# Feeding the FFN: transposes from TensorE to DMA, layer norm on VectorE, both evacuations on ScalarE, another chunk order

## The chip, the cores and the metric

The kernel runs on one core of a Trainium2 chip. Its time is the device time of one execution in microseconds; three executions of the kernel before took 417.68 to 417.83 us, median 417.8. Lower is better. The core's engines are named as in the profile: PE is TensorE (matmuls; PEld its weight loads), DVE is VectorE, ACT is ScalarE, POOL is GpSimd, SP is SyncE, which here only issues DMAs.

## The reference

Two layers of the same pair of blocks over a sequence of 2048 rows of 512 in bf16, each block added to its input:

```python
def _A_ref(q, k, v, shift_k, ssm_k, ssm_D):      # q is the normalised x
    k_shift = sum over t of k_pad[:, t:t + S, :] * shift_k[:, ks - 1 - t]
    kv = k_shift * v
    y = irfft(rfft(kv, 2 * S) * rfft(ssm_k, 2 * S))[:S]      # a long causal convolution
    y = y + kv * ssm_D
    return q * y

def _B_ref(x, w_gate, w_up, w_down):             # F = 1792
    return (silu(x @ w_gate) * (x @ w_up)) @ w_down

x = x + _A_ref(_layernorm(x), A_k, A_v, A_shift_k, A_ssm_k, A_ssm_D)
x = x + _B_ref(_layernorm(x), B_w_gate, B_w_up, B_w_down)
# ... and both once more
```

The convolution's result y depends on k, v and the filter alone, so it is the same in both layers and is computed once.

## The kernel before, in words

The sequence is cut into four chunks of 512 rows (`c`, 0 to 3); a chunk's residual is the tile `xc`, 128 partitions by 4 rows by 512, three buffers. The work on one chunk in one layer is an `ffn(layer, c)`: 14 feature tiles `ft`, each with four gate and four up matmuls (128x128 weights, 512 columns) into two PSUM banks of the tile `pf`, six banks in all, then 4 x 14 down matmuls, whose four results are added to `xc`. ScalarE takes the gate's bank through Silu into `sg`; VectorE multiplies `sg` with the up bank straight out of PSUM into `ht`.

An FFN's input is `zT`, the layer-normalised chunk with features on the partitions. The function `prologue(layer, c)` makes it: it normalises `xc` into `n` (first layer norm, on ScalarE), multiplies by the convolution's result `Y[c]` (the tile `Yk`) and adds to `xc`, takes new statistics (`ln_stats`, on VectorE, with the power of -1/2 on GpSimd), normalises again into `z` (ScalarE), has TensorE transpose the 4 x 4 blocks of `z` into the PSUM tile `ptz`, and ScalarE copies these into `zT`. With `fine` (the first prologue alone) it goes pair of rows by pair of rows.

The convolution is done block by block through 512-point transforms written as matmuls: `spectrum_h(b)` transforms the filter (TensorE transposes `hn` into `pt`, then 16 matmuls into `pc`, two banks), `spectrum_x(b)` the shifted and multiplied input (64 small matmuls with `kTb`, then 16), VectorE forms the products of spectra (`product`, into `Z`), `fold` makes `su` of them, and `inverse(k)` is 16 matmuls on `su` whose results ScalarE copies into `Yk`.

Order: the start-up part is issued as written. From the first `ffn` on, each `ffn` takes steps of its `behind` list after every feature tile (`tick`; `BEHIND` says how many), and a scheduler then puts every engine's instructions into a fixed order ahead of time, which each engine and each DMA queue follows strictly. All loads, stores and the transposing loads of `k` go through SP's queue in order. The `plan` decides which chunk's FFN comes when and what lies behind it.

Of the kernel before, what the change touches and what calls it, by code (L numbers as in the profile page):

```python
# [30 lines left out]
def kernel(  # L31
# [41 lines left out]
    work = tc.alloc_tile_pool(name="work", bufs=2)  # L73
    psp = tc.alloc_tile_pool(name="psp", bufs=1, space=PSUM)
# [29 lines left out]
    wts = {}  # L104
# [17 lines left out]
    ident = const.tile([P, P], BF16, name="ident")  # L122
# [27 lines left out]
    def psf():  # L150
        return psp.tile([P, D], F32, name="pf", bufs=6)
# [4 lines left out]
    def mm(o, terms):  # L156
        for n, (lhsT, rhs) in enumerate(terms):
            nc.tensor.matmul(o, lhsT=lhsT, rhs=rhs, start=(n == 0), stop=(n == len(terms) - 1))  # L158
# [105 lines left out]
    PAIRS = ((0, 2), (1, 3))  # L264

    def fold(Zk, su, sl):
        lo, hi = (slice(0, 2), slice(2, 4)) if sl is None else (sl, sl + 2)
        nc.vector.tensor_add(out=su[:, lo], in0=Zk[:, lo], in1=Zk[:, hi])
        nc.vector.tensor_sub(out=su[:, hi], in0=Zk[:, lo], in1=Zk[:, hi])
# [58 lines left out]

    def normalise(dst, xc, i, o, st):
        rstd, nmr = st  # L330
        nc.scalar.activation(out=dst, in_=xc[:, i, :], func=ACT.Identity, scale=rstd[:, o:o + 1], bias=nmr[:, o:o + 1])  # L331

    zts = {}

    def ln1_stats(layer, c):
        st1[layer, c] = yield from ln_stats_g(xs[c], range(R))
# [3 lines left out]
    def prologue(layer, c, fine=False):  # L340
        xc = xs[c]
        if (layer, c) not in st1:
            yield from ln1_stats(layer, c)
        st = st1.pop((layer, c))
        zT = work.tile([P, KD, R, P], BF16, name="zT", bufs=2)
        zts[layer, c] = zT
        ns = []
        for pair in PAIRS:
            n = work.tile([P, 2, D], BF16, name="n", bufs=2)
            for o, i in enumerate(pair):  # L350
                normalise(n[:, o, :], xc, i, i, st)
            ns.append(n)
        yield

        def transposes(pair, st2):
            pt = psp.tile([P, KD, 2, P], BF16, name="ptz", tag="pc", bufs=2)
            for o, i in enumerate(pair):
                z = work.tile([P, D], BF16, name="z", bufs=2)
                normalise(z[:], xc, i, (o if fine else i), st2)
                for kd in range(KD):  # L360
                    nc.tensor.transpose(pt[:, kd, o, :], z[:, kd * P:(kd + 1) * P], ident[:])  # L361
                yield
            nc.scalar.copy(out=zT[:, :, pair[0]:pair[1] + 1:2, :], in_=pt[:])  # L363
            yield

        for pair, n in zip(PAIRS, ns):
            sl = slice(pair[0], pair[1] + 1, 2)
            nc.vector.tensor_mul(out=n[:], in0=n[:], in1=Y[c][:, sl, :])  # L368
            nc.vector.tensor_add(out=xc[:, sl, :], in0=xc[:, sl, :], in1=n[:])  # L369
            yield  # L370
            if fine:
                yield from transposes(pair, ln_stats(xc, pair))
        if not fine:
            st2 = ln_stats(xc, range(R))
            yield
            for pair in PAIRS:
                yield from transposes(pair, st2)

    def drain(*gens):
        for g in gens:  # L380
            for _ in g:
                pass
# [8 lines left out]
    def ffn(layer, c, behind):  # L391
        steps = NF + R

        def run():
            for g in behind:
                yield from g()
        g = run()
        total = BEHIND[layer, c]
        done = [0, 0]

        def tick():
            done[0] += 1
            while done[1] * (8 if total < 20 else 13) < total * done[0]:
                done[1] += 1
                if next(g, g) is g:
                    break

        xc, zT = xs[c], zts.pop((layer, c))
        hts = []
        for ft in range(NF):  # L410
            pg, pu = psf(), psf()
            mm(pg[:], [(wts["g"][:, kd, ft * P:(ft + 1) * P], zT[:, kd]) for kd in range(KD)])
            mm(pu[:], [(wts["u"][:, kd, ft * P:(ft + 1) * P], zT[:, kd]) for kd in range(KD)])
            sg = work.tile([P, L], BF16, name="sg", bufs=2)
            nc.scalar.activation(out=sg[:], in_=pg[:], func=ACT.Silu)  # L415
            ht = work.tile([P, L], BF16, name="ht", bufs=14)
            nc.vector.tensor_mul(out=ht[:], in0=sg[:], in1=pu[:])  # L417
            hts.append(ht)
            tick()
        for i in range(R):  # L420
            pd = psf()
            mm(pd[:], [(hts[ft][:, i * P:(i + 1) * P], wts["d"][:, ft, :]) for ft in range(NF)])
            nc.vector.tensor_add(out=xc[:, i, :], in0=xc[:, i, :], in1=pd[:])  # L423
# [43 lines left out]
    for par in (0, 1):  # L467
        for _ in product(0, 0, slice(par, 4, 2)):
            if par == 0:
                next(f1)  # L470
        if par == 0:
            prol = prologue(0, 0, True)
            next(prol)
        fold(Z[0], su, par)
    Z.pop(0)
    drain(inverse(0, psf, su), prol)
# [10 lines left out]
    def x_only(b):  # L487
# [51 lines left out]
```

## Time and profile before

| | us |
|---|---|
| median of three executions | 417.8 |
| the profiled execution | 417.13 |
| its span, first to last instruction | 415.3 |
| TensorE busy | 370.3 (89%) |
| VectorE busy | 301.3 (73%) |
| ScalarE busy | 178.7 (43%) |
| GpSimd busy | 19.9 (5%) |

Busy time of TensorE is that of matmuls that overlap in its pipeline: 512 columns show 0.38 us each, while the next one starts 0.216 us later. The mean granted TensorE clock was 0.979. In a row of groups stand the line, the engine, the operation, the tile written and the tiles read, their shapes, the count, then busy time and mean duration, then the engine's idle time just ahead of them and what ended most of it. In a row of the timeline stand start, length, engine, line, operation, tiles, count, and in brackets the idle time ahead.

### The profile page before, as it was taken

Reading aid. Unit: us, or ns where it says so; the run is one execution under the profiler, and the core shown is the slowest. Engines: PE = TensorE matmul, PEld = TensorE weight load, DVE = VectorE, ACT = ScalarE, POOL = GpSimd, SP = SyncE. Lnnn points to the kernel's source line nnn. Section 1 sums busy time; section 2 is a strip of 40 time slices with the busy share of each in tenths; the row PEclk is TensorE's granted clock in tenths of the full one; section 3 lists DMA queues with packets and bytes.
Section 4 is the critical chain, followed back from the end, with each engine's and each line's share of the span. In section 5 each row is a group of like instructions: output and inputs, shape, how many; then the busy total and the mean of one; then the engine's idle time right before and its main releaser. Section 6 shows DMA issues by size and latency. Waiting matters only on the chain.

```text
span 415.3 us, 5086 instructions
## 1 busy us (share of the span) xinstructions
PE 370.3 (89%) x1947; PEld 178.3 (43%) x1984; DVE 301.3 (73%) x504; ACT 178.7 (43%) x281; POOL 19.9 (5%) x27
## 2 busy tenths in 40 slices
PE   2957299888889999989998999999999998999996
PEld 2722164333334644444443634444444443444442
DVE  8797886999794799999999969968233458323331
ACT  4648437231559541429144660475136134602310
POOL 1000100000000000010010000010000000000000
PEclk9988689999999999999999999999999999999999
DMA  8992013000001040000030000000100000000001
GB/s 244 396 290 109 0 20 85 2 0 0 2 0 51 2 104 0 0 2 2 2 101 0 2 0 2 1 2 0 48 4 1 2 0 0 2 25 25 2 13 38
DMA packets 18023, 16.36 MB, mean 39 GB/s; under 512 B 10064, under 2 KB 15952, under 8 KB 18000
## 3 DMA queue, kind: packets, MB, share of 16 engines
q1 hardware_dynamic: 16272, 14.99, 11.6%
q10 hardware_dynamic: 1728, 1.05, 0.9%
q8 instruction: 15, 0.25, 0.2%
q14 instruction: 8, 0.07, 0.0%
HBM read 11.80 MB, written 2.10 MB: 33 GB/s over the span
## 4 chain that ended last, share of the span: by engine, by line
PE 46%; DVE 34%; ACT 8%; issue 5%; DMA 4%; POOL 2%; POOLq 0%; DVEq 0%; ACTq 0%
PE pf L158 38%; PE pc L158 5%; DVE bnst L317 4%; DVE ht L417 4%; DMA hn<-in_A_ssm_k_dram 4%; DVE t L252 3%; DVE t L259 3%; DVE t L250 3%; DVE Z L261 3%; ACT z L331 2%; POOL rstd L323 2%; ACT ev L183 2%; DVE n L368 2%; DVE xc L369 2%; DVE xc L423 1%
## 5 line engine op out<-in xcount | busy, mean ns | idle before, releaser
L415 ACT ACTIVATE sg<-pf 128x512 bf16<-128x512 f32 x112 | 66.4, 597 | 160.9 <-PE pf L158 125.3
L158 PE MATMUL pf<-zT,wg_sb 128*128 128x512 bf16 x435 | 115.9, 380 | 5.7 <-DVE ht L417 4.0
L158 PE MATMUL pf<-zT,wu_sb 128*128 128x512 bf16 x436 | 115.8, 380 | 0.7
L417 DVE TENSOR_TENSOR ht<-sg,pf 128x512 bf16<-128x512 bf16 x112 | 76.5, 684 | 52.7 <-PE pf L158 44.2
L158 PE MATMUL pf<-wd_sb,ht 128*128 128x512 bf16 x438 | 99.8, 379 | 1.5 <-DVE ht L417 0.9
L158 PEld LDWEIGHTS <-ht 128*128 128x128 bf16 x448 | 43.5, 98 | 53.7 <-DVE ht L417 2.4
L158 PEld LDWEIGHTS <-wg_sb 128*128 128x128 bf16 x448 | 43.2, 98 | 53.8 <-issue 7.3
L158 PEld LDWEIGHTS <-wu_sb 128*128 128x128 bf16 x448 | 43.7, 98 | 51.2 <-issue 1.1
L423 DVE TENSOR_TENSOR xc<-xc,pf 128x512 bf16<-128x512 bf16 x32 | 21.5, 687 | 32.5 <-PE pf L158 32.5
L317 DVE BATCH_NORM_STATS2 bnst<-xc 128x6 f32<-128x512 bf16 x64 | 42.3, 682 | 0.3
L323 POOL TENSOR_TENSOR rstd<-ve,nhalf 128x4 f32<-128x4 f32 (+1 forms) x17 | 18.1, 1067 | 330.4 <-DVE ve L321 317.7
L331 ACT ACTIVATE z<-xc,nmr,rstd 128x512 bf16<-128x512 bf16 x32 | 24.6, 806 | 20.7 <-DVE nmr L325 20.2
L183 ACT ACTIVATE ev<-pc 128x512 bf16<-128x512 f32 x48 | 27.0, 611 | 12.0 <-PE pc L158 11.9
L361 PE MATMUL ptz<-ident,z 128*128 128x128 bf16 x128 | 13.5, 232 | 16.2 <-ACT z L331 16.0
L331 ACT ACTIVATE n<-xc,nmr,rstd 128x512 bf16<-128x512 bf16 x32 | 24.9, 821 | 4.7 <-DVE nmr L325 4.7
L250 DVE TENSOR_TENSOR t<-X,G 128x2048 bf16<-128x2048 bf16 (+1 forms) x22 | 24.8, 1127 | 0.1
L252 DVE TENSOR_TENSOR t<-X,G 128x2048 bf16<-128x2048 bf16 (+1 forms) x22 | 24.8, 1126 | 0.0
L158 PEld LDWEIGHTS <-tab_fwd 128*128 128x128 bf16 x128 | 12.8, 101 | 20.6 <-issue 10.1
L361 PEld LDWEIGHTS <-z 128*128 128x128 bf16 x128 | 8.4, 102 | 26.8 <-ACT z L331 24.4
L158 PEld LDWEIGHTS <-kTb 128*128 128x128 bf16 x256 | 18.0, 122 | 2.8 <-issue 1.7
L363 ACT COPY zT<-ptz 128x1024 bf16<-128x1024 bf16 x16 | 16.1, 1004 | 3.1 <-PE ptz L361 3.1
L208 PE MATMUL pt<-ident,hn 128*128 128x128 bf16 x64 | 5.4, 243 | 13.0 <-DVE hn L434 8.3
(61 smaller groups left out, 250.3 us busy)
## 6 DMA issues: line engine op xcount, KB each, us to landing
xc<-in_A_q_dram SPq DMA_DIRECT2D x4, 512.0 KB, 4.5
out_dram<-xc SPq DMA_DIRECT2D x16, 128.0 KB, 1.7
wg_sb<-in_B_w_gate_dram SPq DMA_DIRECT2D x1, 1792.0 KB, 10.6
wu_sb<-in_B_w_up_dram SPq DMA_DIRECT2D x1, 1792.0 KB, 14.7
wd_sb<-in_B_w_down_dram SPq DMA_DIRECT2D x1, 1792.0 KB, 20.0
hn<-in_A_ssm_k_dram SPq DMA_DIRECT2D x3, 512.0 KB, 6.7
vt<-in_A_v_dram SPq DMA_DIRECT2D x3, 512.0 KB, 3.4
hn<-in_A_ssm_k_dram ACTq DMA_DIRECT2D x1, 512.0 KB, 3.6
```

Of the source, the lines that this page charges most:

```text
L158: nc.tensor.matmul(o, lhsT=lhsT, rhs=rhs, start=(n == 0), stop=(n == len(terms) - 1))
L183: nc.scalar.activation(out=ev[:, slot, part], in_=ps[:], func=ACT.Copy, scale=scale)
L250: nc.vector.tensor_mul(out=t1[:], in0=Xi[:, sl, 0, :], in1=Gj[:, sl, part, :])
L252: nc.vector.tensor_mul(out=t2[:], in0=Xi[:, sl, 1, :], in1=Gj[:, sl, 1 - part, :])
L317: nc.vector.bn_stats(out=st[:], in_=xc[:, i, :])
L323: nc.gpsimd.tensor_tensor(out=rstd[:], in0=ve[:], in1=nhalf[:].to_broadcast((P, n)), op=ALU.pow)
L331: nc.scalar.activation(out=dst, in_=xc[:, i, :], func=ACT.Identity, scale=rstd[:, o:o + 1], bias=nmr[:, o:o + 1])
L361: nc.tensor.transpose(pt[:, kd, o, :], z[:, kd * P:(kd + 1) * P], ident[:])
L363: nc.scalar.copy(out=zT[:, :, pair[0]:pair[1] + 1:2, :], in_=pt[:])
L415: nc.scalar.activation(out=sg[:], in_=pg[:], func=ACT.Silu)
L417: nc.vector.tensor_mul(out=ht[:], in0=sg[:], in1=pu[:])
L423: nc.vector.tensor_add(out=xc[:, i, :], in0=xc[:, i, :], in1=pd[:])
```

## The change

Four edits:

- `normalise` runs as a TENSOR_SCALAR on VectorE in place of an ACTIVATE on ScalarE, for `n` and `z` alike (32 of each in all). `n` is made pair by pair with one buffer.
- Except in the first prologue, `zT` is no longer made by TensorE and ScalarE: SP issues a transposing DMA from SBUF to SBUF for each of the four rows of `z` (28 in all, 128 KB each).
- In the FFN, ScalarE evacuates both banks, the gate's through Silu into `sg`, the up's by a copy into `ht`; VectorE multiplies two feature tiles at once, in bf16 out of SBUF, in place.
- The plan's order is (0,0), (0,1), (1,0), (1,1), (0,2), (0,3), (1,2), (1,3); before it was (0,2) ahead of (1,1). The steps behind the FFNs are dealt out anew, 40 for each of the first five.

```diff
     def normalise(dst, xc, i, o, st):
         rstd, nmr = st
-        nc.scalar.activation(out=dst, in_=xc[:, i, :], func=ACT.Identity, scale=rstd[:, o:o + 1], bias=nmr[:, o:o + 1])
+        nc.vector.tensor_scalar(out=dst, in0=xc[:, i, :], scalar1=rstd[:, o:o + 1], scalar2=nmr[:, o:o + 1],
+                                op0=ALU.mult, op1=ALU.add)
...
-        ns = []
-        for pair in PAIRS:
-            n = work.tile([P, 2, D], BF16, name="n", bufs=2)
-            for o, i in enumerate(pair):
-                normalise(n[:, o, :], xc, i, i, st)
-            ns.append(n)
-        yield
-
         def transposes(pair, st2):
-            pt = psp.tile([P, KD, 2, P], BF16, name="ptz", tag="pc", bufs=2)
+            if fine:
+                pt = psp.tile([P, KD, 2, P], BF16, name="ptz", tag="pc", bufs=2)
             for o, i in enumerate(pair):
                 z = work.tile([P, D], BF16, name="z", bufs=2)
                 normalise(z[:], xc, i, (o if fine else i), st2)
-                for kd in range(KD):
-                    nc.tensor.transpose(pt[:, kd, o, :], z[:, kd * P:(kd + 1) * P], ident[:])
+                if fine:
+                    for kd in range(KD):
+                        nc.tensor.transpose(pt[:, kd, o, :], z[:, kd * P:(kd + 1) * P], ident[:])
+                else:
+                    nc.sync.dma_start_transpose(out=zT[:, :, i, :], in_=z[:].rearrange("p (k f) -> p k f", k=KD))
                 yield
...
-        for pair, n in zip(PAIRS, ns):
+        for pair in PAIRS:
             sl = slice(pair[0], pair[1] + 1, 2)
+            n = work.tile([P, 2, D], BF16, name="n", bufs=1)
+            for o, i in enumerate(pair):
+                normalise(n[:, o, :], xc, i, i, st)
...
-        for ft in range(NF):
-            pg, pu = psf(), psf()
...
-            sg = work.tile([P, L], BF16, name="sg", bufs=2)
-            nc.scalar.activation(out=sg[:], in_=pg[:], func=ACT.Silu)
-            ht = work.tile([P, L], BF16, name="ht", bufs=14)
-            nc.vector.tensor_mul(out=ht[:], in0=sg[:], in1=pu[:])
+        for f0 in range(0, NF, 2):
+            sg = work.tile([P, 2, L], BF16, name="sg", bufs=2)
+            ht = work.tile([P, 2, L], BF16, name="ht", bufs=7)
+            for o, ft in enumerate((f0, f0 + 1)):
+                pg, pu = psf(), psf()
...
+                nc.scalar.activation(out=sg[:, o, :], in_=pg[:], func=ACT.Silu)
+                nc.scalar.copy(out=ht[:, o, :], in_=pu[:])
+                tick()
+            nc.vector.tensor_mul(out=ht[:], in0=ht[:], in1=sg[:])
...
     plan = [
         ((0, 0), [g_(x_only, 1), g_(spectrum_x, 1), g_(conv_products, 1), g_(inverse, 1),
-                  g_(prologue, 0, 1), g_(loads, 2), g_(eager, 1)]),
-        ((0, 1), [g_(prologue, 1, 0), g_(spectrum_h, 2), g_(spectrum_x, 2), g_(conv_products, 2)]),
+                  g_(prologue, 0, 1), g_(loads, 2)]),
+        ((0, 1), [g_(prologue, 1, 0), g_(eager, 1), g_(spectrum_h, 2), g_(spectrum_x, 2)]),
-        ((1, 0), [g_(inverse, 2), g_(prologue, 0, 2), g_(loads, 3), g_(eager, 2), g_(spectrum_h, 3)]),
-        ((0, 2), [g_(prologue, 1, 1), g_(spectrum_x, 3), g_(conv_products, 3), g_(inverse, 3)]),
-        ((1, 1), [g_(prologue, 0, 3)]),
+        ((1, 0), [g_(prologue, 1, 1), g_(conv_products, 2), g_(eager, 2), g_(loads, 3)]),
+        ((1, 1), [g_(inverse, 2), g_(prologue, 0, 2), g_(spectrum_h, 3), g_(spectrum_x, 3)]),
+        ((0, 2), [g_(conv_products, 3), g_(inverse, 3), g_(prologue, 0, 3)]),
...
-    BEHIND = {(0, 0): 55, (0, 1): 49, (1, 0): 45, (0, 2): 44, (1, 1): 10, (0, 3): 10, (1, 2): 10, (1, 3): 1}
+    BEHIND = {u: 40 for u, _ in plan}
+    BEHIND.update({(0, 3): 10, (1, 2): 10, (1, 3): 1})
```

What this does to the fixed orders shows at three places. The first is VectorE near the end of the first FFN, (0,0), where the products for chunk 1 end in `su`, on which TensorE's inverse waits. A row gives line, operation, tile written and tiles read, shape, and in brackets the counters that it waits for (DVE, PE, Activation for an engine, DMAHW for a DMA). Before:

```order
L259 TENSOR_TENSOR t_721<-t_721,t_722 128x2048 [waits DVE_49]
L417 TENSOR_TENSOR ht<-sg,pf 128x512 [waits PE_49,Activation_49]
L261 TENSOR_TENSOR Z<-Z,t_721 128x4x512 [waits DVE_49]
L417 TENSOR_TENSOR ht<-sg,pf 128x512 [waits PE_49,Activation_49]
L268 TENSOR_TENSOR su<-Z 128x2048 [waits DVE_49]
L269 TENSOR_TENSOR su<-Z 128x2048
```

and now:

```order
L259 TENSOR_TENSOR t_746<-t_746,t_747 128x2048 [waits DVE_49]
L261 TENSOR_TENSOR Z<-Z,t_746 128x4x512 [waits DVE_49]
L250 TENSOR_TENSOR t_1122<-X_624,G_520 128x2048
L268 TENSOR_TENSOR su<-Z 128x2048 [waits DVE_49]
L269 TENSOR_TENSOR su<-Z 128x2048
L421 TENSOR_TENSOR ht<-ht,sg 128x1024 [waits Activation_49]
```

Fewer products stand between the spectra's rows, a row of a later product has come ahead of `su`, and the seventh and last pair of feature tiles stands behind `su`. In TensorE's list, 13 of the first FFN's down matmuls now stand ahead of the inverse of chunk 1 and 43 behind it; behind these stand block 2's filter transposes, 16 filter matmuls and 27 of its shift matmuls, and only then the first gate matmul of (0,1). Before, five down matmuls stood ahead of the inverse, and block 2's spectrum came after the start of (0,1).

The second place is VectorE where `z` of chunk 1 is made, from the fourth of the residual adds (L426) that end (0,0). Now:

```order
L426 TENSOR_TENSOR xc<-xc,pf 128x512 [waits PE_49]
L331 TENSOR_SCALAR z<-xc,rstd,nmr 128x512 [waits DVE_49]
L331 TENSOR_SCALAR z<-xc,rstd,nmr 128x512
L318 BN_AGGR mv<-bnst 128x2 x2
L317 BN_STATS bnst<-xc 128x6
L317 BN_STATS bnst<-xc 128x6 [waits DVE_49]
L318 BN_AGGR mv<-bnst 128x2 [waits DVE_49]
L252 TENSOR_TENSOR t_1143<-X_624,G_520 128x2048
L318 BN_AGGR mv<-bnst 128x2 [waits DVE_49]
L256 TENSOR_TENSOR Z<-t_1142,t_1143 128x4x512 [waits DVE_49]
L331 TENSOR_SCALAR z<-xc,rstd,nmr 128x512 [waits DMAHW2_49]
L331 TENSOR_SCALAR z<-xc,rstd,nmr 128x512 [waits DMAHW3_49]
```

The first two `z` stand behind that add, which waits for the last down matmul of (0,0), and the last two wait for the DMAs that read the two `z` buffers. Before, `z` was ScalarE's, which does no residual add:

```order
L331 ACTIVATE z<-xc,nmr,rstd 128x512 [waits DVE_49]
L331 ACTIVATE z<-xc,nmr,rstd 128x512
L331 ACTIVATE z<-xc,nmr,rstd 128x512 [waits PE_49,Activation_49]
L363 COPY zT<-ptz 128x8x128 [waits PE_49]
L331 ACTIVATE z<-xc,nmr,rstd 128x512 [waits Activation_49]
```

There the third `z` waited for TensorE's transposes; now it waits for a DMA, and VectorE's other work stands behind it. The third place is SP's queue around these DMAs, chunk 1's first four transposes, then chunk 0's for the second layer. Before, block 3's loads followed each other:

```order
L82 DMA hn<-in_A_ssm_k_dram 128x4x512 [waits DMAHW6_49,PE_49]
L91 DMA_TRANSPOSE kTb<-in_A_k_dram 128x4x528 [waits DMAHW7_49,PE_49]
L96 DMA vt<-in_A_v_dram 128x2048 [waits DMAHW0_49,DMAHW3_49,DVE_49,PE_49]
L425 DMA out_dram<-xc 128x512 [waits DMAHW4_49,DVE_49]
L425 DMA out_dram<-xc 128x512 [waits DVE_49] x3
```

and now:

```order
L82 DMA hn<-in_A_ssm_k_dram 128x4x512 [waits DMAHW6_49,PE_49]
L358 DMA_TRANSPOSE zT<-z 128x4x128 [waits DVE_49]
L358 DMA_TRANSPOSE zT<-z 128x4x128 [waits DMAHW3_49,DVE_49]
L358 DMA_TRANSPOSE zT<-z 128x4x128 [waits DMAHW4_49,DVE_49]
L358 DMA_TRANSPOSE zT<-z 128x4x128 [waits DVE_49]
L358 DMA_TRANSPOSE zT<-z 128x4x128 [waits DVE_49,Activation_49]
L358 DMA_TRANSPOSE zT<-z 128x4x128 [waits DMAHW7_49,DVE_49]
L358 DMA_TRANSPOSE zT<-z 128x4x128 [waits DMAHW0_49,DVE_49]
L358 DMA_TRANSPOSE zT<-z 128x4x128 [waits DMAHW1_49,DVE_49]
L91 DMA_TRANSPOSE kTb<-in_A_k_dram 128x4x528 [waits DMAHW2_49,PE_49]
L96 DMA vt<-in_A_v_dram 128x2048 [waits DMAHW3_49,DVE_49,PE_49]
```

Eight transposes of `z` now stand between the load of block 3's filter, which waits for TensorE, and the loads of its `k` and `v`.

More of the change, by code (lines that the diff above doesn't have):

```diff
@@ L359, in transposes @@
                 normalise(z[:], xc, i, (o if fine else i), st2)
-                for kd in range(KD):
-                    nc.tensor.transpose(pt[:, kd, o, :], z[:, kd * P:(kd + 1) * P], ident[:])
+                if fine:
[3 more added lines that the diff above has]
+                    nc.sync.dma_start_transpose(out=zT[:, :, i, :], in_=z[:].rearrange("p (k f) -> p k f", k=KD))
                 yield
-            nc.scalar.copy(out=zT[:, :, pair[0]:pair[1] + 1:2, :], in_=pt[:])
-            yield
-        for pair, n in zip(PAIRS, ns):
+            if fine:
+                nc.scalar.copy(out=zT[:, :, pair[0]:pair[1] + 1:2, :], in_=pt[:])
+                yield
+        for pair in PAIRS:
             sl = slice(pair[0], pair[1] + 1, 2)
+            n = work.tile([P, 2, D], BF16, name="n", bufs=1)
+            for o, i in enumerate(pair):
+                normalise(n[:, o, :], xc, i, i, st)
             nc.vector.tensor_mul(out=n[:], in0=n[:], in1=Y[c][:, sl, :])
@@ L472 @@
             prol = prologue(0, 0, True)
-            next(prol)
         fold(Z[0], su, par)
```

7 lines of the change are left out of this document (3 added, 4 removed).

## The prediction

> **What bounds the kernel now.** I read the page first, then busy time by stage, then TensorE's rows in order of time, then the waits. A stage here is one chunk's FFN, from its first gate matmul to the next one's; the 52.9 us ahead are start-up.
>
> ```profile
> span 415.3 us, 5086 instructions
> PE 370.3 (89%) x1947; PEld 178.3 (43%) x1984; DVE 301.3 (73%) x504; ACT 178.7 (43%) x281; POOL 19.9 (5%) x27
> ...
> core 0: us, PE busy (x) PEld busy (x) DVE busy (x) ACT busy (x) POOL busy (x), PEclk, DMA share, GB/s
> 52.90:108.20 55.30, 49.23 (x264) 23.23 (x269) 49.10 (x67) 22.10 (x36) 2.01 (x2) 0.98 0.08 20
> 108.20:160.30 52.10, 49.53 (x291) 24.66 (x297) 40.82 (x69) 28.34 (x46) 3.02 (x3) 1.00 0.12 32
> 160.30:208.70 48.40, 45.96 (x230) 21.01 (x233) 47.37 (x61) 20.74 (x34) 1.82 (x1) 1.00 0.00 1
> 208.70:256.90 48.20, 45.44 (x261) 22.20 (x265) 43.17 (x73) 22.51 (x36) 3.83 (x3) 1.00 0.07 22
> 256.90:299.00 42.10, 40.66 (x197) 18.79 (x200) 29.21 (x60) 19.21 (x30) 3.02 (x3) 1.00 0.03 10
> 299.00:336.20 37.20, 36.99 (x182) 17.34 (x185) 15.02 (x24) 11.70 (x18) 0.00 (x0) 1.00 0.01 5
> 336.20:375.40 39.20, 37.19 (x181) 17.17 (x184) 18.78 (x36) 15.35 (x24) 2.01 (x2) 1.00 0.03 11
> 375.40:415.30 39.90, 36.28 (x166) 16.34 (x167) 13.08 (x19) 8.36 (x14) 0.00 (x0) 1.00 0.05 17
> ```
>
> The stages are, in order, (0,0), (0,1), (1,0), (0,2), (1,1), (0,3), (1,2), (1,3), each named (layer, chunk). From 299 us on TensorE is the limit: a stage lasts as long as its matmuls. In the first four VectorE is busy 41 to 49 us of 48 to 55, nearly as full as TensorE; the two wait for each other in turn. To count what is lost I need TensorE's issue time for each piece of work, which I take from one row's start to the next:
>
> ```profile
> 57.68 1.95 PE L158 MATMUL pc<-dg,kTb 128*128 128x128 bf16 x32
> 59.68 0.81 PE L158 MATMUL pf<-zT,wu_sb 128*128 128x512 bf16 x3
> ...
> 260.25 3.61 PE L158 MATMUL pc<-su,tab_inv 128*128 128x512 bf16 x16 [0.41 <-DVE su L268]
> 263.70 0.81 PE L158 MATMUL pf<-zT,wu_sb 128*128 128x512 bf16 x3
> ...
> 311.13 0.39 PE L361 MATMUL ptz<-ident,z 128*128 128x128 bf16 x4
> 311.35 0.81 PE L158 MATMUL pf<-zT,wg_sb 128*128 128x512 bf16 x3
> ...
> 411.88 0.69 DVE L423 TENSOR_TENSOR xc<-xc,pf 128x512 bf16<-128x512 bf16 x1 [2.33 <-PE pf L158]
> ```
>
> 16 wide matmuls take 3.45 us (0.216 each), 32 shift matmuls 2.0, four z transposes 0.22, so a chunk's 16 cost 0.9. Stage (0,3) is 37.2 with 0.9 of transposes: one FFN is 36.3. The work behind the first stage's start: 8 x 36.3, three inverses (10.35), two h spectra (16 transposes 0.9 and 16 wide: 8.7), three x spectra (6.75, 7.45, 7.45; 10 of the first one's 64 shift matmuls are in start-up): 331.1. With seven chunks' z transposes (6.3) it is 337.4, and the stages up to the last residual add at 411.9 take 359.0. So 21.6 us are lost: 7.9 in (0,0), 3.1, 3.4 and 3.6 in the next three, 1.4, 0, 2.0 and about 0.2 in the rest.
>
> **ScalarE, VectorE and TensorE: prices.**
>
> ```profile
> L415 ACT ACTIVATE sg<-pf 128x512 bf16<-128x512 f32 x112 | 66.4, 597 | 160.9 <-PE pf L158 125.3 <-DVE ht L417 27.3 <-DVE mv L318 3.8
> L417 DVE TENSOR_TENSOR ht<-sg,pf 128x512 bf16<-128x512 bf16 x112 | 76.5, 684 | 52.7 <-PE pf L158 44.2 <-ACT sg L415 6.8 <-PE ptz L361 1.4
> L290 ACT CAST Yk<-pc 128x512 bf16<-128x512 f32 x12 | 7.0, 586 | 5.8 <-PE pc L158 5.8
> L331 ACT ACTIVATE n<-xc,nmr,rstd 128x512 bf16<-128x512 bf16 x32 | 24.9, 821 | 4.7 <-DVE nmr L325 4.7
> L331 ACT ACTIVATE z<-xc,nmr,rstd 128x512 bf16<-128x512 bf16 x32 | 24.6, 806 | 20.7 <-DVE nmr L325 20.2 <-PE ptz L361 0.5
> L363 ACT COPY zT<-ptz 128x1024 bf16<-128x1024 bf16 x16 | 16.1, 1004 | 3.1 <-PE ptz L361 3.1
> L368 DVE TENSOR_TENSOR n<-n,Yk 128x1024 bf16<-128x1024 bf16 x16 | 11.1, 693 | 6.0 <-ACT Yk L290 3.6 <-ACT n L331 2.3
> L321 DVE TENSOR_SCALAR ve<-mv 128x4 f32<-128x4 f32 x15 | 2.6, 171 | 0.3
> L145 DVE TENSOR_SCALAR ph<-ph 128x1536 int32<-128x1536 int32 x2 | 1.9, 961 | 0.1
> L181 DVE TENSOR_SCALAR evx<-pf 128x512 bf16<-128x512 f32 x4 | 2.6, 684 | 0.0
> ```
>
> *Evacuation.* A gate-up product was 0.684 us of VectorE for 512 columns, reading PSUM; in pairs it has the shape of L368, 0.693 for 1024. VectorE: 112 products (76.5) become 56 (38.8), 37.7 less. ScalarE gains 112 copies like L290: 112 x 0.586 = 65.6. It needs 1.2 us per feature tile against 8 x 0.216 = 1.73 on TensorE, so beside it; and a PSUM bank no longer waits for VectorE, only `ht` does, which the down matmuls read 2 to 3 us after the last gate.
>
> *Layer norm.* ScalarE sheds 24.9 + 24.6; VectorE gets 64 TENSOR_SCALARs. No row has that shape from SBUF in bf16. Bounds: 0.17 (L321, hardly any data) and 0.68 (L181, same shape out of PSUM). L145 moves 1365 elements of 4 bytes more than L321 covers in 0.79 us, 0.58 ns each; half that for 2 bytes gives 0.17 + 512 x 0.29 = 0.32. I take 0.3, nearest to L145's reading: 19 us. VectorE ends at 301.3 - 37.7 + 19 = 283, ScalarE at 178.7 + 65.6 - 49.5 - 14 x 1.0 = 181. Neither total is the bound; what matters is VectorE's order in the first stages.
>
> *Transposes.* 112 of 128 leave TensorE (6.3 us, in the sum above) and 14 of L363 leave ScalarE. SP gets 28 DMA transposes.
>
> ```profile
> kTb<-in_A_k_dram SPq DMA_TRANSPOSE x4, 5.3
> out_dram<-xc SPq DMA_DIRECT2D x16, 128.0 KB, 1.7
> 144.88 1.87 SPq L91 DMA_TRANSPOSE kTb<-in_A_k_dram  x1
> DMA to landing us min/median/max: 4.4/5.3/11.4
> ```
>
> A transpose of four times these bytes lands 4.4 us after issue when undisturbed and holds SP 1.87; a plain store of the same 128 KB takes 1.7. Those are the bounds. A quarter of the 1.87 is 0.47 of SP; the landing is nearer the row of equal size: 2.1 to 2.3, and the second of a pair 2.8. I take 2.8. With two `z` buffers, VectorE's third `z` waits for the first transpose, and all rows behind it wait too.
>
> SP's queue is served in order. Ahead of chunk 1's transposes stands block 3's `hn` load, which waits until TensorE has transposed block 2's `hn`: in the new order right behind (0,0)'s down matmuls, 1 us before the first `z` is ready. Its 3.5 us lie ahead of the first transpose on the DMA engines, which then lands up to 2 us later; the third `z` isn't due before.
>
> ```profile
> hn<-in_A_ssm_k_dram SPq DMA_DIRECT2D x1, 512.0 KB, 3.5
> ```
>
> [...] No run here shows an SBUF source yet.
>
> **Where a wait stays, by stage.**
>
> ```profile
> 87.59 1.23 DVE L268 TENSOR_TENSOR su<-Z 128x2048 bf16<-128x2048 bf16 x1
> 88.73 1.23 DVE L269 TENSOR_TENSOR su<-Z 128x2048 bf16<-128x2048 bf16 x1
> 107.09 1.01 ACT L363 COPY zT<-ptz 128x1024 bf16<-128x1024 bf16 x1 [0.49 <-PE ptz L361]
> 108.16 1.02 PE L158 MATMUL pf<-zT,wg_sb 128*128 128x512 bf16 x3 [1.10 <-ACT zT L363]
> ...
> PE pf L158 <- DVE ht L417: 4.9, 6, 2.1
> ACT sg L415 <- DVE ht L417: 27.3, 16, 4.0
> DVE nmr L325 <- POOL rstd L323: 7.6, 9, 1.2
> ```
>
> (The last three rows are of 52.9 to 260 us.) VectorE's rows issue about 0.09 us closer than they last, as the two `su` show. My prices for its rows in the new order are therefore 1.15 for a 2048-wide one, 0.6 for a product, an add or a statistic, 0.3 for a normalise, 0.1 for the small ones.
>
> (0,0): start-up is taken as unchanged: ScalarE's `n` no longer stand ahead of the first `Yk` copies (1 us sooner), VectorE's `n` and `z` take it back. `su` of chunk 1 ended at 90.0 on VectorE. Ahead of it now: 11 products less (6.6), 6 pairs (3.6), one early 2048-row (1.15), two `n` (0.6), and 0.6 from start-up: 89.3. The seventh pair stands behind `su`, 89.9, and TensorE's 13th down matmul waits for it. Then inverse (3.45) and 43 down matmuls (9.3): TensorE ends the stage's own work at 102.8. On VectorE, the rows from the pair to that stage's fourth residual add (3 wide, 14 of 0.6, 2 normalise, 6 small: 13.1) plus waits for `Yk` (1.6) and `rstd` (0.7) end at 105.3, and that add stands ahead of the `z`. Two `z` 0.6, other rows 3.9, two `z` 0.6: 110.4; plus 2.8: the gate starts at 113.2. TensorE covers part with 6.0 us of chunk 2's spectrum, which ScalarE's eight 0.6 copies stretch to about 9. Length 60.3, work 52.45: **7.9 lost**, as before.
> (0,1): from those `z` to its last pair VectorE has 16 wide rows, 19 of 0.6, 8 normalise, 8 small (33.0), and about 4 of waits (`rstd` twice, 0.85 each by the row above, and `ev` of the x spectrum): 147.4. TensorE wants that pair after 24.2 of gates, 5.75 of spectrum and 12 down matmuls, 2.6: 145.7. A shift product that TensorE waits for may cost part of that before; together **1.8 lost**, next gate at 157.05 (36.3 + 5.75 + 1.8).
> (1,0): TensorE has no convolution work here, VectorE the heaviest share: 18 wide rows, 23 of 0.6, 8 normalise, 12 small (38.1) and 2.4 of waits put its last pair at 187.9; TensorE wants it at 157.05 + 24.2 + 2.6 = 183.8. **4.1 lost**, next gate at 197.5.
> (1,1) has an inverse, an h and an x spectrum, no less than the stages that lost 3.1 to 3.6, and VectorE waits for two spectra within it: **3.1**. From (0,2) on VectorE has under half a stage's work, its last transposes are issued some 12 us before the next gate, and no `z` transpose stands in TensorE's queue to wait for VectorE: **0.3** for four stages. There even a landing of 11.4 would be covered.
>
> Sum: 52.9 + 331.1 + 17.2 = 401.2; the tail of 3.4 (last add, store) stays: span 404.6. Against 415.3 that is 6.3 of transposes and 4.4 of waits. The profiled execution lies 1.8 over its span (417.1) and the median 0.7 over that (417.8): **407**.
>
> **Rivals.**
> 1. *Slow transposes, ending slower.* If an SBUF source costs far more on SP, VectorE blocks on the third `z` in four early stages. Between the pairs stand 4.0, 2.4, 2.9 and about 1.4 us of other rows, so each us over 3 costs about 3.5. The 10.7 gained are gone at 2.8 + 10.7 / 3.5 = 5.9 us per transpose. At the 11.4 us that one k transpose took beside the weights: 407 + 8.6 x 3.5 = 437. For: 28 issues of a kind not seen. Against: 4.4 undisturbed with four times the bytes. 0.14.
> [...]
> 2. *TENSOR_SCALAR at L181's speed.* About 24 of them in the first three stages, 0.38 more each: 9 us, 416; near no change. For: nearest row in shape. Against: that row reads PSUM. 0.06.
> 3. *Waits shrink too.* If VectorE's rows wait less for each other than I allow, (1,0) loses nothing and (0,0) some 3 less: 400. For: 27.3 us of ScalarE waiting for products goes. 0.14.
> 4. *Nothing gained*, the stage order giving back what the transposes free: 417. 0.04.
>
> My forecast holds 0.62. Its range, with landings of 1.7 to 4.4 us (-2 to +5) and (1,0) as it may be, is 402 to 413; with rival 3 and half of 2, 398 to 415. Faster by over 0.2% (about what a measurement of this kernel can tell from no change): 0.82; within it 0.04; slower 0.14.
>
> **What would show it.** No transpose of z behind the start-up on TensorE; paired products of 0.69, normalise rows of 0.3, transposes landing in 2 to 3 us; TensorE's longest gap before gate (0,1) at about 113, a second of some 4 in (1,0)'s down matmuls; the last four stages at 36.3 to 40. Wrong, if VectorE's waits on DMA sum to over 10 us, or if SP's queue is late with a transpose behind a load that waits.

## The result and the profile after

The changed kernel takes 408.0 us (median of four runs, 407.4 to 409.2) where the kernel before took 417.8: ratio 0.977, 95% interval 0.974 to 0.979. The profiled execution took 407.4, its span is 405.6. First the busy times of its page, then those by stage; the stages are now (0,0), (0,1), (1,0), (1,1), (0,2), (0,3), (1,2), (1,3).

```profile
PE 363.0 (89%) x1837; PEld 173.9 (43%) x1872; DVE 290.0 (72%) x512; ACT 186.8 (46%) x315; POOL 19.7 (5%) x27
```

```profile
core 0: us, PE busy (x) PEld busy (x) DVE busy (x) ACT busy (x) POOL busy (x), PEclk, DMA share, GB/s
53.00:114.20 61.20, 54.03 (x307) 26.75 (x313) 53.38 (x83) 29.08 (x50) 3.02 (x3) 0.99 0.15 36
114.20:158.07 43.87, 41.99 (x216) 20.04 (x222) 39.74 (x58) 20.64 (x36) 1.85 (x1) 1.00 0.18 37
158.07:201.00 42.93, 39.16 (x167) 16.99 (x169) 37.94 (x65) 15.62 (x28) 3.56 (x3) 0.92 0.09 22
201.00:253.54 52.54, 51.66 (x292) 25.60 (x296) 45.03 (x71) 28.44 (x50) 2.09 (x3) 1.00 0.10 28
253.54:293.25 39.71, 39.50 (x181) 17.99 (x184) 22.15 (x41) 18.89 (x32) 1.01 (x1) 1.00 0.09 21
293.25:329.51 36.26, 36.10 (x166) 16.46 (x168) 19.80 (x43) 16.47 (x28) 2.01 (x2) 1.00 0.07 15
329.51:365.77 36.26, 36.05 (x165) 16.42 (x168) 17.17 (x37) 16.24 (x28) 2.01 (x2) 1.00 0.14 26
```

The five stages that hold convolution work were 246.1 us together and are 240.3; the last three and the tail were 116.3 and are 112.3. With 0.1 us more of start-up that is the 9.7 by which the span shrank. Five chunks' transposes (0.9 each) lay in the first group and two in the second, 6.3 in all; the other 3.4 are waits, less what a lowered clock costs in (1,0), below. (0,3) and (1,2) are at 36.26, one FFN without a gap. Nearly all that is still lost stands in (0,0), (0,1) and (1,0), and (1,0) has a granted clock of 0.92.

The groups that answer to the prediction's prices, on ScalarE and VectorE:

```profile
L419 ACT CAST ht<-pf 128x512 bf16<-128x512 f32 x112 | 65.7, 586 | 27.2 <-PE pf L158 27.0
L421 DVE TENSOR_TENSOR ht<-ht,sg 128x1024 bf16<-128x1024 bf16 x56 | 38.1, 683 | 35.4 <-ACT ht L419 35.3
L331 DVE TENSOR_SCALAR z<-xc,rstd,nmr 128x512 bf16<-128x512 bf16 x32 | 12.1, 408 | 10.0 <-DMA zT<-z 9.9
L331 DVE TENSOR_SCALAR n<-xc,rstd,nmr 128x512 bf16<-128x512 bf16 x32 | 12.0, 407 | 0.3
```

The transposes: what one holds of SP's queue (minimum, median and maximum in ns), and its landing, minimum, median and maximum:

```profile
L358 SPq DMA_TRANSPOSE zT<-z x28: 1188/1206/2078, 105.0 to 349.4; - x28
...
DMA to landing us min/median/max: 2.4/2.5/4.5
```

And TensorE's rows (with the wait ahead of a row in brackets) around its three longest waits behind the start-up, with VectorE's row that the third of them waits for:

```profile
85.66 2.97 PE L158 MATMUL pf<-wd_sb,ht 128*128 128x512 bf16 x13
89.49 3.61 PE L158 MATMUL pc<-su,tab_inv 128*128 128x512 bf16 x15 [0.86 <-DVE su L268]
...
114.22 1.02 PE L158 MATMUL pf<-zT,wg_sb 128*128 128x512 bf16 x3 [2.81 <-DMA zT<-z]
135.63 0.38 PE L158 MATMUL pc<-vt,tab_fwd 128*128 128x512 bf16 x1 [1.60 <-DVE vt L230]
188.78 12.35 PE L158 MATMUL pf<-wd_sb,ht 128*128 128x512 bf16 x43 [3.39 <-DVE ht L421]
```

```profile
109.02 0.73 DVE L331 TENSOR_SCALAR z<-xc,rstd,nmr 128x512 bf16<-128x512 bf16 x2
...
188.04 0.69 DVE L421 TENSOR_TENSOR ht<-ht,sg 128x1024 bf16<-128x1024 bf16 x1
```

The longest is the seventh pair's in (1,0). The 43 down matmuls behind it take 12.35 us; at 0.216 each they should take 9.45. The stretches of 2 us there show why (TensorE's busy time, then its granted clock):

```profile
184.00:186.00 2.00, 1.17 (x5) 1.00 0.64 128
186.00:188.00 2.00, 0.00 (x0) 0.85 0.30 60
188.00:190.00 2.00, 1.22 (x3) 0.50 0.41 84
190.00:192.00 2.00, 2.00 (x6) 0.50 0.00 0
192.00:194.00 2.00, 2.00 (x6) 0.50 0.18 62
194.00:196.00 2.00, 2.00 (x10) 0.94 0.01 4
```

The clock falls to 0.50 near the end of the wait and is back at about 194: a wait of 3.4 us that costs 6.3.

### The profile page after: what moved, and what is told of

Same layout as the page of the kernel before. It is cut to its first block, busy times and chain, and to the rows that moved or that the text cites. A ratio compares the mean times of both kernels' runs of the same rounds, so it can differ in the third digit from the quotient of the medians.

```text
span 405.6 us, 4831 instructions
## 1 busy us (share of the span) xinstructions
PE 363.0 (89%) x1837; PEld 173.9 (43%) x1872; DVE 290.0 (72%) x512; ACT 186.8 (46%) x315; POOL 19.7 (5%) x27
## 4 chain that ended last, share of the span: by engine, by line
PE 53%; DVE 38%; ACT 2%; POOL 2%; issue 2%; DMA 2%; POOLq 0%; DVEq 0%
PE pf L158 49%; DVE t L252 5%; DVE t L250 5%; PE pc L158 4%; DVE bnst L317 3%; DVE ht L421 3%; DVE Z L256 2%; DVE Z L261 2%; POOL rstd L323 2%; DVE t L259 2%; DVE vt L230 2%; DMA zT<-z 2%; DVE xc L426 1%; ACT ev L183 1%; DVE ph L143 1%
## 5 line engine op out<-in xcount | busy, mean ns | idle before, releaser
L158 PE MATMUL pf<-zT,wu_sb 128*128 128x512 bf16 x439 | 114.0, 379 | 0.4
L419 ACT CAST ht<-pf 128x512 bf16<-128x512 f32 x112 | 65.7, 586 | 27.2 <-PE pf L158 27.0
L421 DVE TENSOR_TENSOR ht<-ht,sg 128x1024 bf16<-128x1024 bf16 x56 | 38.1, 683 | 35.4 <-ACT ht L419 35.3
L426 DVE TENSOR_TENSOR xc<-xc,pf 128x512 bf16<-128x512 bf16 x32 | 21.8, 681 | 30.9 <-PE pf L158 30.9
L331 DVE TENSOR_SCALAR z<-xc,rstd,nmr 128x512 bf16<-128x512 bf16 x32 | 12.1, 408 | 10.0 <-DMA zT<-z 9.9
L158 PE MATMUL pc<-hs,tab_fwd 128*128 128x512 bf16 x47 | 14.8, 424 | 2.9 <-ACT hs L209 1.8
L208 PE MATMUL pt<-ident,hn 128*128 128x128 bf16 x64 | 5.7, 260 | 12.8 <-DVE hn L437 8.3
L158 PE MATMUL pc<-vt,tab_fwd 128*128 128x512 bf16 x47 | 12.9, 378 | 2.8 <-DVE vt L230 2.8
L261 DVE TENSOR_TENSOR Z<-Z,t 128x2048 bf16<-128x2048 bf16 x12 | 14.6, 1218 | 0.2
## 6 DMA issues: line engine op xcount, KB each, us to landing
wg_sb<-in_B_w_gate_dram SPq DMA_DIRECT2D x1, 1792.0 KB, 10.4
```

Of the source, the lines that this page charges most:

```text
L261: nc.vector.tensor_add(out=Zk[:, sl, part, :], in0=Zk[:, sl, part, :], in1=t1[:])
L331: nc.vector.tensor_scalar(out=dst, in0=xc[:, i, :], scalar1=rstd[:, o:o + 1], scalar2=nmr[:, o:o + 1], op0=ALU.mult, op1=ALU.add)
L419: nc.scalar.copy(out=ht[:, o, :], in_=pu[:])
L421: nc.vector.tensor_mul(out=ht[:], in0=ht[:], in1=sg[:])
```

## Experiments

### One part undone

Four kernels put one part of the change back and leave the others.

*Transposes on TensorE again* (with ScalarE's copy):

```diff
-            if fine:
+            if True:
                 pt = psp.tile([P, KD, 2, P], BF16, name="ptz", tag="pc", bufs=2)
...
-                if fine:
+                if True:
                     for kd in range(KD):
```

> The changed kernel with the z transposes of all eight chunks on TensorE and the copy of their result on ScalarE again; everything else as changed. Theory A (the prediction's sum): 112 transposes cost TensorE 6.3 us, and since TensorE or a wait for the next chunk sets every stage, nearly all of it counts; the wait of 2.8 us for the DMA transpose ahead of gate (0,1) shrinks to about 1, and the granted clock's loss in stage (1,0) stays: 408 + 6.3 - 1.8 = 412.5 (411 to 415). Rival B (the transposes stood in time in which TensorE waited anyway, as in the first four stages): only the four of the late stages count, 4 x 0.9 = 3.6, less 1.8: 410 or less.

Measured: 425.0 us (423.0 to 426.5), 17.0 over the changed kernel and slower than the kernel before, ratio 1.017 (1.014 to 1.021). Both expectations are far too low. Of the 15.6 us that its span gained (the profiled execution is its fastest), 5.2 stand ahead of gate (0,2), 10.4 in the rest, where VectorE has under half a stage's work. Rows of stage (0,3):

```profile
313.08 1.01 POOL L323 TENSOR_TENSOR rstd<-ve,nhalf 128x4 f32<-128x4 f32 x1 [8.86 <-DVE ve L321]
...
314.32 0.73 DVE L331 TENSOR_SCALAR z<-xc,rstd,nmr 128x512 bf16<-128x512 bf16 x2
314.79 0.40 PE L356 MATMUL ptz<-ident,z 128*128 128x128 bf16 x4 [2.81 <-DVE z L331]
```

TensorE has gate matmuls to do, but the transpose stands ahead of them in its queue, and `z` waits for a chain of small rows over two engines. So 2.81 us go in the middle of the gates, here and again at 354.93, and each of these two stages takes 40.1 us where the changed kernel takes 36.3, though its transposes last 0.9. What the DMA takes off TensorE is first of all a row that waits.

*The old order* (plan and steps per stage of the kernel before):

```diff
-    BEHIND = {u: 40 for u, _ in plan}
+    BEHIND = {(0, 0): 55, (0, 1): 49, (1, 0): 45, (0, 2): 44, (1, 1): 10, (0, 3): 10, (1, 2): 10, (1, 3): 1}
```

> The changed kernel with the plan (which convolution steps and prologues stand behind which chunk's FFN, chunk order, steps per stage) of the kernel before. Theory A (the prediction gave the order no term of its own; the gain is transposes and relieved VectorE): within 3 us of the changed kernel, 405 to 411. Rival B (the order is what lets the relief pay): 412 or more. Rival C: the new order costs time, since it puts the heaviest VectorE load behind stage (1,0), which has no convolution work for TensorE, so that the 3.4 us wait and the lowered clock after it (3.1 us) go with it: 402 or less.

Measured: 412.3 us (411.7 to 412.9), 4.2 more, ratio 0.986 (0.984 to 0.988). Rival B: the order is worth some 4 us beside the other parts, for which the prediction had no term. Its stage (1,0) isn't free of the wait either; TensorE stops 3.54 us there for ScalarE's `ev`.

*Normalise on ScalarE again:*

```diff
-        nc.vector.tensor_scalar(out=dst, in0=xc[:, i, :], scalar1=rstd[:, o:o + 1], scalar2=nmr[:, o:o + 1],
-                                op0=ALU.mult, op1=ALU.add)
+        nc.scalar.activation(out=dst, in_=xc[:, i, :], func=ACT.Identity, scale=rstd[:, o:o + 1], bias=nmr[:, o:o + 1])
```

> The changed kernel with the layer norm's normalise rows on ScalarE again (64 rows of 0.81 us there instead of 64 rows 0.32 apart on VectorE). VectorE has some 20 us less, ScalarE some 52 more, 239 of 405. Theory A (VectorE's order bounds the first stages): the wait in stage (1,0) shortens by the 8 rows there, 2.6 us, and with it the lowered clock goes; but z comes 0.5 later per row at gate (0,1): 403 to 408. Rival B (ScalarE, which now evacuates gate and up, becomes the queue that z and the PSUM banks wait in): 410 or more.

Measured: 420.8 us (420.6 to 421.1), 12.8 more: rival B's direction, but half of it lies elsewhere. Gate (0,0) starts at 59.3, not 53.0:

```profile
56.91 0.60 PE L355 MATMUL ptz<-ident,z 128*128 128x128 bf16 x4 [8.69 <-ACT z L331]
```

The kernel before, with ScalarE's `z` too, waits 3.89 there (50.45). It normalised both pairs' `n` first; the changed code writes the second pair's `n` behind the first pair's `z`, which suits VectorE and not ScalarE. So 6.3 of the 12.8 lie in the start-up, where that order of lines explains them (ScalarE makes the second pair's `n` at 49.2, behind the first pair's `z` at 46.0; no run moved these lines alone), and about 6.5 come with the engine in the later stages.

*The product from PSUM again* (`ht` = `sg` times the up bank, one tile at a time):

```diff
-                nc.scalar.copy(out=ht[:, o, :], in_=pu[:])
...
-            nc.vector.tensor_mul(out=ht[:], in0=ht[:], in1=sg[:])
+            nc.vector.tensor_mul(out=ht[:], in0=sg[:], in1=pu[:])
```

> The changed kernel with the gate-up product read from PSUM by VectorE again, 112 rows of 0.684 us in place of 56 of 0.69 and 112 ScalarE copies. Theory A (VectorE bounds the first four stages): each of these gets 14 rows of 0.6 more on VectorE and a PSUM bank that waits for VectorE; at least 5 us each where VectorE is full, in three to four stages: 408 + 15 to 25 = 423 to 433, slower than the kernel before. Rival B (the copy is hidden and so was the product; the gain is the transposes): 408 to 412.

Measured: 412.3 us (410.8 to 413.9), only 4.3 more, at the edge of rival B and far from theory A, though VectorE is busy 322.1 us, 32 more. Stage (0,0) ends at 114.20 as in the changed kernel, and (1,0) is even shorter, 39.2 for 42.9: VectorE's lateness shows there as two short waits, 0.71 and 1.39, and not one long one, and no lowered clock follows: the 11 and 6 matmuls behind them last 2.53 and 1.47 us, 0.22 apart. What it loses stands elsewhere: (0,1) is 46.9 for 43.9, with a granted clock of 0.50 from 114.20 to 116.20, behind a wait of 2.59, and (1,1) is 56.8 for 52.6.

```profile
186.12 2.53 PE L158 MATMUL pf<-wd_sb,ht 128*128 128x512 bf16 x11 [0.71 <-DVE ht L418]
190.05 1.47 PE L158 MATMUL pf<-wd_sb,ht 128*128 128x512 bf16 x6 [1.39 <-DVE ht L418]
```

### One part alone

Three kernels make one part of the change in the kernel before.

*DMA transposes alone* (`if fine:` ahead of TensorE's transposes and the copy, `else` the DMA):

> The kernel before with one part of the change alone: z transposed by DMA (seven chunks), normalise still on ScalarE, product still from PSUM, old order. Theory A (the transposes carry most of the gain wherever they are taken off TensorE, their own 6.3 us and the waits for z and zT that stood in TensorE's queue, 10.7 us in the profile of before, less about 3 per exposed landing): 405 to 411. Rival B (it pays only together with normalise on VectorE, since ScalarE's z come late in a queue of evacuations, and the landing of 2.5 us and the SP issue of 1.2 us come on top): 414 or more.

Measured: 411.5 us (410.9 to 413.2), ratio 0.985 (0.982 to 0.989): 6.6 us gained against the kernel before as timed beside it (418.06). The time lies just above theory A's range, and the gain is about the 6.3 that the transposes last.

*Evacuation alone* (the FFN's lines as changed, `n` in one buffer and in the changed place):

> The kernel before with the paired evacuation alone (gate and up by ScalarE, 56 products of 1024 columns on VectorE); normalise on ScalarE, transposes on TensorE, old order; the n tile is single-buffered, as in the changed kernel. ScalarE 178.7 + 65.6 = 244, VectorE 264. Theory A (VectorE's relief pays about what undoing it cost, 4 us): 411 to 416. Rival B (ScalarE's queue, which now carries evacuations and the 64 normalise rows, holds up z and n, as in the run with normalise back on ScalarE, which lost 12.8): 420 or more.

Measured: 428.3 us (427.6 to 429.7), 10.3 slower than the kernel before, ratio 1.025 (1.022 to 1.028): rival B. It has the same start-up loss as the run with normalise on ScalarE (gate (0,0) at 59.3, TensorE's wait again 8.69), and at gate (0,1) `z` and `zT` come late from a ScalarE that is busy 238.8 us:

```profile
111.63 1.31 PE L355 MATMUL ptz<-ident,z 128*128 128x128 bf16 x8 [2.64 <-ACT z L331]
...
117.41 1.87 PE L158 MATMUL pf<-zT,wg_sb 128*128 128x512 bf16 x4 [1.98 <-ACT zT L360]
```

The start-up, with the moved `n` as above, is 6.4 of its 10.3; behind it the evacuation loses about 4.

*Normalise on VectorE alone:*

> The kernel before with one part alone: the layer norm's normalise rows on VectorE (64 rows 0.32 apart, 20.5 us), product from PSUM, transposes on TensorE, old order. Theory A (VectorE is as full as TensorE in the first four stages, some 40 of the 64 rows stand there, 13 us): 422 to 430. Rival B (ScalarE's z were late behind its evacuations, and VectorE gives them sooner): 412 to 418.

Measured: 417.8 us (416.9 to 418.1, ten runs), ratio 0.999 (0.998 to 1.000): rival B's upper end. VectorE's busy time rose from 301.3 to 320.9 and the time did not move. Together with the product from PSUM (322.1 busy, 4.3 us more) it says that VectorE's total does not set this kernel's time.

The parts don't add: alone they change the time by -6.6 (transposes), +10.3 (evacuation) and -0.1 (normalise); undone they cost 17.0, 4.3 and 12.8. Two of these, +10.3 and 12.8, hold the start-up's 6.3 to 6.4; without it they are about +4 and 6.5. Evacuation by ScalarE pays once ScalarE is rid of the normalise rows. Why undoing the transposes costs more than making them alone gains is shown only in part. In (0,3), where TensorE's transposes wait for `z`, the stage takes 40.1 us with normalise, evacuation and order all changed. With TensorE's transposes it takes 37.2 in the kernel with normalise alone changed, and 37.2 in the one with evacuation alone. So neither of these two makes the transposes wait by itself; which combination does was not tried.

### The price of an issue

*Each transpose cut into four of 128x128:*

```diff
-                    nc.sync.dma_start_transpose(out=zT[:, :, i, :], in_=z[:].rearrange("p (k f) -> p k f", k=KD))
+                    for k0 in range(0, KD, 1):
+                        nc.sync.dma_start_transpose(out=zT[:, k0:k0 + 1, i, :],
+                                                    in_=z[:, k0 * P:(k0 + 1) * P].rearrange("p (k f) -> p k f", k=1))
```

> The changed kernel with each 128x512 DMA transpose cut into four of 128x128, the same bytes in four issues. Theory A (SP's 1.2 us belongs to each issue): SP holds 4.8 us per z, its last piece lands some 6 us after the first issue; by the prediction's slope of 3.5 us for each us over 3 that is 408 + 3 x 3.5 = 418.5, and more where the waits lower the clock. [...]

*One transpose of 128x1024 for a pair of rows* (`z` holds the pair, in one buffer; `zT`'s slots 2k + o lie evenly spaced):

```diff
+                    normalise(z2[:, :, o, :], xc, i, i, st2)
+                    if o == 1:
+                        nc.sync.dma_start_transpose(out=zT[:].rearrange("f k r p -> f (k r) p")[:, pair[0]:KD * R:2, :],
+                                                    in_=z2[:].rearrange("p k o f -> p (k o) f"))
```

> The changed kernel with one DMA transpose of 128x1024 for a pair of rows in place of two of 128x512 (14 issues for 28; z is one buffer of two rows). Theory A (the split run gave the issue a fixed price, 1.2 to 1.3 us of SP and 2.4 to 2.5 to landing for 128x128 as for 128x512): at twice the elements it lands in about 3 us, gate (0,1) starts at 112.8 where it was 114.2, and the wait there is 1.4 and not 2.8: 405 to 407.5. Rival B (from 128x512 up the price goes by elements, so 2.4 of SP and 4.5 to landing): 408 to 409.5. Rival C (with one buffer VectorE's third z waits for the whole landing at every boundary, and what stands behind it too): 410 or more.

Measured: split 465.7 us (463.8 to 467.4), pairs 406.2 (404.2 to 407.4). The issues of both and their landing, read as before; of the split kernel also how long VectorE waited for them and how often:

```profile
L359 SPq DMA_TRANSPOSE zT<-z x112: 1094/1230/2258, 105.0 to 412.1; - x112
...
  DVE z L331: 62.8, 14
...
DMA to landing us min/median/max: 2.2/2.4/4.2
```

```profile
L363 SPq DMA_TRANSPOSE zT<-z x14: 1232/1232/1510, 105.8 to 349.2; - x14
...
DMA to landing us min/median/max: 3.0/3.1/4.8
```

128x128, 128x512 and 128x1024 hold SP 1.23, 1.21 and 1.23 us: the price belongs to the issue, theory A in both runs, while the landing grows from 2.4 over 2.5 to 3.1. Pairs shorten the wait at gate (0,1) from 2.81 to 1.24. The split kernel fell much further than its 418.5: VectorE waits 62.8 us for transposes, and what stands behind the waiting row is late in the last stages too (TensorE waits 4.22 and 5.19 us there for ScalarE's `sg`), where I had counted nothing.

### The wait in (1,0) and the clock behind it

*VectorE's products of chunks 1 and 2 moved out of (1,0)*; then *half of them moved*, then that *with the pair transposes*. (They are 14 wide rows, not the eight of the expectations: six that make a new `Z` and eight that add to it.)

```diff
-        ((1, 0), [g_(prologue, 1, 1), g_(conv_products, 2), g_(eager, 2), g_(loads, 3)]),
+        ((1, 0), [g_(prologue, 1, 1), g_(conv_products, 2), g_(loads, 3)]),
...
-        ((0, 2), [g_(conv_products, 3), g_(inverse, 3), g_(prologue, 0, 3)]),
+        ((0, 2), [g_(eager, 2), g_(conv_products, 3), g_(inverse, 3), g_(prologue, 0, 3)]),
```

> The changed kernel with one step of the plan moved: the eight wide VectorE products of chunks 1 and 2 (eager, 2) stand behind stage (0,2), at its head, and no longer behind (1,0). Theory A (the loss in (1,0) is VectorE's last pair, 3.4 us late, plus the granted clock of 0.5 for some 6.8 us after that wait, 3.1 us): with 8 x 1.15 = 9.2 us less on VectorE there, both go: 408 - 6.5 = 401.5, and (0,2), where VectorE is busy 22 of 40 us, takes them for 0 to 2: 401 to 404. Rival B (the wait moves to (1,1) or (0,2), whose inverse waits for these products): 406 or more. Rival C (the slow matmuls after the wait are not due to the wait): the wait goes, 3.1 us of slow matmuls stay somewhere: 404.5.

Measured: 414.2 us (412.7 to 415.9). Within (1,0) theory A holds: the stage is 36.26 long (161.17 to 197.43), the wait and the slow matmuls are gone together, and rival C with them. But (0,2) becomes 49.2 for 39.7, rival B:

```profile
277.41 3.61 PE L158 MATMUL pc<-su,tab_inv 128*128 128x512 bf16 x16 [2.03 <-DVE su L268]
298.98 1.86 PE L158 MATMUL pf<-zT,wg_sb 128*128 128x512 bf16 x4 [7.16 <-DMA zT<-z]
```

VectorE is half idle in (0,2), yet products, fold, inverse, residual, statistics, `z` and transposes are one chain there that ends when the next gate is due. Idle time of an engine isn't room for a row at the head of a chain.

```diff
+        ((1, 0), [g_(prologue, 1, 1), g_(conv_products, 2), g_(product, 1, 2), g_(loads, 3)]),
...
+        ((1, 1), [g_(inverse, 2), g_(prologue, 0, 2), g_(spectrum_h, 3), g_(spectrum_x, 3), g_(product, 2, 1)]),
```

> The changed kernel with half of what the run before moved: of the eight wide products of chunks 1 and 2, four stay behind (1,0) and four go to the end of what stands behind (1,1). Theory A (VectorE is 3.4 us late in (1,0); the lowered clock after that wait costs 3.1): 4 x 1.15 = 4.6 us less there takes both, (1,0) is 36.3 long, and (1,1), where VectorE is busy 45 of 52.5 us, takes the four for 0 to 1.5: 401 to 404.5. Rival B (the chain in (0,2), products, fold, inverse, prologue, has no slack, as in the run that moved all eight, and starts later by these rows): what (1,0) gives comes back ahead of gate (0,3): 406 to 411.

Measured: 408.0 us (407.2 to 410.0), no change, for a reason that neither theory had. The eight moved rows do start later on VectorE, at 186.63 for 174.55, but the scheduler filled their place with the fold's two wide rows and four statistics rows that had stood behind the seventh pair, and the first two of the eight still stand ahead of the seventh pair, which starts at 188.94 for 188.04:

```profile
186.63 1.19 DVE L250 TENSOR_TENSOR t<-X,G 128x2048 bf16<-128x2048 bf16 x1
187.74 0.17 DVE L321 TENSOR_SCALAR ve<-mv 128x4 f32<-128x4 f32 x1
187.81 1.22 DVE L252 TENSOR_TENSOR t<-X,G 128x2048 bf16<-128x2048 bf16 x1
188.94 0.69 DVE L421 TENSOR_TENSOR ht<-ht,sg 128x1024 bf16<-128x1024 bf16 x1
```

> The last two edits together, the pair transposes and the half move. Theory A (independent, each with its own wait): 408 - 1.5 - 5.5 = 401 (399 to 403). Rival B (the plan's move gives nothing): as the pair transposes alone, 405 or more.

Measured: 405.6 us (405.4 to 407.3), ratio 0.971 (0.969 to 0.974) against the changed kernel's 0.977 (0.974 to 0.979): faster than both kernels, by the pair transposes; theory A's second half didn't come about. Its (1,0) still has a wait of 3.68 us.

## Why the prediction came out as it did

The time came 1.0 us above the forecast, and so did the span (405.6 for 404.6). The 6.3 us of transposes and most places of the waits were right; that the sum came so close is in part luck, since errors of 1 to 3 us in (0,0), (1,0) and (1,1) cancel.

- *Prices on the engines.* Pair 0.68 (0.69), copy 0.586 (0.586). A normalise row lasts 0.41, not 0.3; but two in a row end 0.73 after the first starts, so they issue 0.32 apart, and the sums needed that distance. The 0.3 was worked out as a duration and fits the distance by luck. (Its working has a slip: L145 covers 1532 elements more than L321, not 1365, which gives 0.30 for its 0.32.) VectorE's busy total is 290 and not 283 mostly for this.
- *Transposes.* Removed: 6.3 us of TensorE, as taken. The landing of one, 2.5 us, lies within the bounds, but SP's share was mis-sized: a quarter of the `k` transpose's 1.87 was taken, 0.47, and it is 1.2, since the price goes by the issue (1.23, 1.21 and 1.23 us for 128x128, 128x512 and 128x1024). The gate so starts 4.5 us behind chunk 1's last `z` (109.75 to 114.22), not 2.8. About half of the difference is that price. The other half is a single issue: the third transpose held SP 2.08 us, the longest of the 28, so the fourth was issued at 111.58 and landed at 114.08; why, the runs don't show. VectorE was 0.65 early; gate (0,1) came 1.0 late.
- *(0,0).* TensorE's thirteenth down matmul was to wait for the seventh pair. It doesn't: that matmul ran at 88.25, ahead of the pair (90.49), so it already belongs to another residual row, and TensorE waited 0.86 for `su`. Its own work ended as forecast, at 102.2 (102.8).
- *(0,1).* 43.85 forecast, 43.85 measured. The loss is a shift product (1.60), not the last pair: of the two causes named it is the second, and the size is right by luck, since the 1.7 of the first didn't come.
- *(1,0).* The wait was where forecast, 3.39 for 4.1, but it is the longest and the one at gate (0,1) the second, not the other way round. The lowered clock, 2.9 us, was in no term.
- *(1,1).* 52.5 for 54.65: of the 3.1 allowed for waits, taken by likeness to other stages, 1.0 came. This pays back most of (1,0)'s clock.
- *Late stages.* 39.71, 36.26 and 36.26, within 0.1. VectorE's waits for transposes sum to 9.9 us over the kernel, 8.7 of it behind 201 us, where TensorE waits for none. That is just under the 10 that the prediction named as a sign of being wrong.
- *Rival 1's slope* of 3.5 us for each us over 3 was far too flat: in the split kernel a row's last piece lands 6.1 us after its first issue (3 x 1.23 + 2.4), for which the slope gives 407 + 3.1 x 3.5 = 418; it took 465.7, five times the loss. The break-even of 5.9 us was therefore too generous; the forecast stood because the landing was short.
- *What the sum had no place for:* that the parts depend on each other. The order's 4 us, and an evacuation that loses alone (10 us, about 4 of them behind the start-up) and gains 4 among the others, had no terms.

## What to carry to other kernels

Ask of a step that another engine feeds not how long it lasts but what stands behind it in its queue: in two late stages 0.9 us of transposes cost TensorE 3.9, and a DMA made them free. Price a small transposing DMA by the issue (1.2 us of SP here, from 128x128 to 128x1024), and merge issues as long as what that saves exceeds the longer landing (3.1 us for 2.5). And test a change of several parts by undoing each and by making each alone, since here one part alone lost time and the whole gained 10 us; ask of each such run which other lines it moved.

## What was not expected of the hardware

In these runs TensorE's granted clock falls to 0.50 after some waits of a few us and not after others. The place is gate (0,1), first in the changed kernel after a wait of 2.81 us, then in the kernel with the product from PSUM after one of 2.59. Each row is a stretch of 3.41 us, with TensorE's busy time and its granted clock:

```profile
112.33:115.74 3.41, 1.47 (x7) 1.00 0.19 38
115.74:119.16 3.42, 3.42 (x17) 1.00 0.00 0
```

```profile
110.46:113.87 3.41, 1.15 (x21) 1.00 0.72 77
113.87:117.28 3.41, 3.08 (x8) 0.50 0.00 0
117.28:120.70 3.42, 3.42 (x18) 1.00 0.00 0
```

The longer wait left the clock alone and the shorter one did not. What separates them is where the wait lies. In the trace of the changed kernel the clock changes 4, 6, 9, 12, 51 and 53 times 3.41 us after its first change, in that of the kernel before 4, 6, 9 and 12 times: only at the edges of windows of that length. Behind the start-up it fell at the end of windows in which TensorE stood idle for 2.25 us (changed kernel, 184.00 to 187.42) and 2.26 (product from PSUM, the first row above), and not of those with 1.94 (changed kernel, 112.33 to 115.74) and 1.87 (kernel before, 82.46 to 85.87). It stayed low through a window with 1.36 idle (changed kernel, 187.42 to 190.83), and was back after the next one, with none, and after one with 0.33 (product from PSUM, 113.87 to 117.28). The wait of 2.81 straddles two windows, 0.92 and 1.89 of it in each; that of 2.59 has 2.26 in one. So the length alone doesn't decide: by these figures, as an estimate, a single wait under 1.9 us costs nothing more, one over 4.5 (twice 2.25) lowers the clock wherever the edges fall, and between them it goes by where they fall. The four executions of the changed kernel had mean granted clocks of 0.962 to 0.971 and took 407.4 to 409.2 us. That the edges fall at another place in each execution was not shown; if they do, kernels with such waits can differ, as an estimate, by 1.5 to 3 us (half of the 3.08 above; 12.35 for 9.45 in (1,0)) without any difference in their own work.

The windows are read off the traces: no run shifted a wait against them on purpose, and no variant of the changed kernel without the wait in (1,0) and at gate (0,1) at once was found.
